# Expert lists of 832 slots, filled by indirect row writes and read transposed, in a chunked-attention and mixture-of-experts kernel

## The chip, the cores and the metric

The kernel runs on one core of one Trainium2 chip. The metric is the time of one execution on the device in microseconds; the kernel before has a median of 394.88 us over three runs (394.33 to 395.27). The core has five engines that run their own instruction streams and wait for each other through semaphores: PE (matrix products into PSUM), DVE and ACT (elementwise work, and the only way out of PSUM), POOL (here mainly the issue of DMAs, among them all indirect ones and all that convert types) and SP (the issue of plain DMAs). All DMAs share 16 DMA engines.

## What is computed

Two stages follow each other. First, attention over chunks of 32 positions with a context of 16 to the left and 8 to the right and 8 memory rows, for 4 batches, 8 heads, 768 positions, 64 channels. Its output, seen as 3072 rows of 512, is the input `x` of a mixture of 8 experts, of which each row uses two.

```
for c in range(nc):                                   # 24 chunks
    k_full = concat([mem_k, k[:, :, l_start:r_end]]); v_full = likewise
    a = softmax(scale * q_c @ k_full^T)
    out[:, :, c_start:c_end] = a @ v_full
...
noisy_logits = x @ w_gate + log1p(exp(x @ w_noise)) * noise
top2 = the two largest of 8; top2_w = softmax over the two
for e in range(E):
    h = relu(x[rows of e] @ w1[e])                    # 512 -> 1024
    out[rows of e] += top2_w * (h @ w2[e])            # 1024 -> 512
```

## The kernel before

The program is written in the order in which each engine executes it (`manual_schedule`); an engine takes its instructions strictly in that order.

**Attention.** It runs over 16 pairs of heads (4 batches of 4 pairs). Loop iteration `i` (L462) works on several pairs at once: transposes of `q` and `k` for pair `i+2` (`qkT_pe`, L206), scores for `i+1`, softmax for `i`, the product with `v` for `i-1` (`PV_pe`, L273), its normalised result written into the row tile `xrow` of the batch (`mult_dve`, L286, L294), transposes of those rows and router logits for `i-2` and `i-3`. The row tile has two buffers, so batch `b` reuses the one of batch `b-2`. The loads of `q`, `k`, `v` (L109, L118) go out on POOL in groups of two pairs, two groups ahead, each into one of three buffers; after the last group POOL issues the first three weight loads (`w1` and `w2` of expert 0, `w1` of expert 1: L439, L444). A weight load reads 2 MB of f32 and writes 1 MB of bf16.

**Routing.** For each batch, `route(b)` (L320) finds the two experts of each row with 8 x 8 comparisons, and counts rows by unordered pair of experts: 28 buckets of up to 128 rows. The rank of a row in its bucket comes from products with a triangular and an all-ones matrix (L368 to L373). One-hot products (L395, L409) turn ranks into a table of row numbers, 128 per bucket. Rows that find no place (rank over 127) go to a spill list of 32, and beyond that to a closing loop (L738) that runs all experts over 128 rows at a time. The rows of each batch, with 8 gate values behind them, are written once to DRAM (`x_rows`, L385, on SP).

**Experts.** A row is gathered once, by bucket (`gather`, L578, an indirect DMA on POOL), transposed on PE (`turn`, L585) and copied into `xTb`, where it stays for both of its experts. Expert `e` uses the seven buckets that contain it: a first product of 32 x (512 + 416) columns (L644), relu shared between ACT and DVE (L630, L632), a second product per bucket of 8 matmuls of 512 columns (L652). The first expert of a bucket stores its scaled result in an SBUF accumulator (L656), the second adds to it on DVE (L659) and writes the 128 rows to `out` by an indirect DMA (L660). The weights of expert `e+2` are issued during expert `e`; `w1` and `w2` have three buffers each. After the last write the closing loop is entered zero times for this input, and the program ends.

## Time and profile before

| What | us |
|---|---|
| median of three runs | 394.88 |
| span of the profiled execution, first to last instruction | 393.1 |
| PE busy | 304.5 (77%) |
| DVE busy | 169.9 (43%) |
| POOL busy | 124.5 (32%) |
| ACT busy | 119.8 (30%) |
| DMA moved | 42.93 MB, 109 GB/s on average |

The profile is one execution on the chip. "Busy" counts the time in which an engine executes, not its waits. A row of the order-of-time view gives start, duration, engine, line, operation and tiles, the number of merged instructions, and in brackets the idle time before it with what ended that. "SPq" and "ACTq" rows are the issue of DMAs. The clock column is the share of PE's full clock that was granted. Times are microseconds from the span's start.

### The profile page before, as it was taken

To read this page: it belongs to the slowest core of one execution; us is meant where nothing else is said; L and a number is where in the kernel's file an instruction comes from. 1 tells how busy PE (TensorE), PEld (TensorE's weight loads), DVE (VectorE), ACT (ScalarE), POOL (GpSimd) and SP (SyncE) were. 2 spreads that over 40 slices of the span, in tenths; PEclk is the share of its full clock that TensorE was granted. 3 is DMA by queue.
4 is the path that set the end of the run, shared out by engine and by line. 5 is a ranking of instruction groups with operands and counts; after the bars stand their busy time and mean duration, and the time that the engine had idled before them with its cause. 6 is when DMAs were issued, how large, how long until landed. Compare 5 with 4: busy or idle time off the path is not lost.

```text
span 393.1 us, 9217 instructions
## 1 busy us (share of the span) xinstructions
PE 304.5 (77%) x4042; PEld 188.6 (48%) x4060; DVE 169.9 (43%) x350; ACT 119.8 (30%) x235; POOL 124.5 (32%) x143
## 2 busy tenths in 40 slices
PE   0448688676846433888998998999998999999990
PEld 0436566454634322654465474454454454544540
DVE  7426345787757761342142242241433242443340
ACT  1436354565532200222333232233221312302200
POOL 7766234265000026352100420520605123032061
PEclk9999555898885655699999999999999999999997
DMA  9999999999970412849700291291492921811021
GB/s 92 100 164 156 158 152 94 167 150 141 211 154 3 143 46 80 151 82 216 141 0 2 45 221 30 64 209 34 97 213 88 191 56 71 132 67 70 3 115 59
DMA packets 83324, 42.93 MB, mean 109 GB/s; under 512 B 57255, under 2 KB 76711, under 8 KB 83280
## 3 DMA queue, kind: packets, MB, share of 16 engines
q0 software_dynamic: 74928, 38.85, 70.6%
q1 hardware_dynamic: 8064, 3.38, 3.4%
q8 instruction: 34, 0.56, 0.6%
q10 hardware_dynamic: 288, 0.07, 0.1%
q14 instruction: 10, 0.08, 0.1%
HBM read 61.32 MB, written 10.65 MB: 183 GB/s over the span
## 4 chain that ended last, share of the span: by engine, by line
PE 60%; DVE 15%; issue 10%; DMA 7%; ACT 3%; POOL 3%; POOLq 0%; DVEq 0%; ACTq 0%
PE ps_h L644 24%; PE ps_y L652 21%; DMA x_rows<-xrow 4%; PE p_t L216 3%; DMA kg<-in_k_dram 2%; PE ps_o L279 2%; PE ps_o L282 2%; DVE xrow L294 2%; PE p_t L589 2%; DVE vg L130 2%; DVE xTb L590 2%; POOL out_dram L660 2%; DVE mx L251 1%; ACT qT L218 1%; PE p_x L303 1%
## 5 line engine op out<-in xcount | busy, mean ns | idle before, releaser
L644 PE MATMUL ps_h<-xTb,w1t 128*128 128x512 bf16 (+3 forms) x608 | 107.8, 328 | 1.1 <-DVE xTb L590 1.0
L652 PE MATMUL ps_y<-w2t,ht 128*128 128x512 bf16 x430 | 98.9, 379 | 1.0 <-issue 0.2
L644 PEld LDWEIGHTS <-w1t 128*128 128x128 bf16 x864 | 64.7, 98 | 45.0 <-issue 1.1
L632 DVE TENSOR_SCALAR ht<-ps_h 128x416 bf16<-128x416 f32 (+2 forms) x68 | 41.7, 613 | 81.0 <-PE ps_h L644 81.0
L660 POOL DMA_INDIRECT out_dram<-acc,sidx x28 | 28.0, 998 | 144.9 <-DVE acc L659 142.4
L652 PEld LDWEIGHTS <-ht 128*128 128x128 bf16 x448 | 42.3, 98 | 48.9
L630 ACT ACTIVATE ht<-ps_h 128x416 bf16<-128x416 f32 (+2 forms) x68 | 36.3, 535 | 87.2 <-PE ps_h L644 83.1
L580 POOL DMA_INDIRECT xl<-x_rows,gidx x28 | 29.1, 1038 | 71.4 <-DVE ov1b L523 48.4
L644 PE MATMUL ps_h<-xTs,w1t 128*128 128x32 bf16 x256 | 45.4, 177 | 0.2 <-DVE xTs L605 0.2
L118 POOL DMA_DIRECT2D vg<-in_v_dram x34 | 32.9, 974 | 35.4 <-PE ps_o L282 29.8
L656 ACT ACTIVATE acc<-ps_y,meta 128x512 f32<-128x512 f32 x28 | 19.2, 687 | 76.5 <-PE ps_y L652 47.7
L659 DVE SCALAR_TENSOR_TENSOR acc<-ps_y,meta,acc 128x512 f32<-128x512 f32 x28 | 21.0, 751 | 38.6 <-PE ps_y L652 38.6
L590 DVE COPY xTb<-p_t 128x512 bf16<-128x512 bf16 x28 | 11.8, 423 | 27.1 <-PE p_t L589 26.9
L218 ACT CAST qT<-p_t 128x384 bf16<-128x384 f32 x32 | 16.9, 586 | 20.2 <-PE p_t L216 20.2
L216 PE MATMUL p_t<-identb,kg 128*64 128x128 bf16 x192 | 14.1, 275 | 10.5 <-ACT qT L218 7.7
L251 DVE TENSOR_REDUCE mx<-ps_s 128x12 f32<-128x768 f32 x16 | 15.2, 950 | 12.1 <-PE ps_s L243 12.1
L305 ACT COPY xt<-p_x 128x768 bf16<-128x768 bf16 x16 | 12.8, 799 | 22.5 <-PE p_x L303 22.5
L216 PE MATMUL p_t<-identb,qg 128*64 128x128 bf16 x192 | 11.5, 265 | 9.5 <-DMA qg<-in_q_dram 5.1
L279 PE MATMUL ps_o<-memv,PT 128*128 128x132 bf16 x96 | 11.2, 273 | 9.4 <-DVE PT L270 9.4
L589 PE MATMUL p_t<-identb,xl 128*128 128x128 bf16 x112 | 11.2, 224 | 8.9 <-DVE xTb L590 8.9
L218 ACT CAST kT<-p_t 128x384 bf16<-128x384 f32 x32 | 17.0, 597 | 2.0 <-PE p_t L216 1.7
L294 DVE TENSOR_TENSOR xrow<-ps_o,rec 128x768 bf16<-128x768 f32 x16 | 15.3, 958 | 5.3 <-DMA x_rows<-xrow 4.8
(128 smaller groups left out, 295.5 us busy)
## 6 DMA issues: line engine op xcount, KB each, us to landing
w1t<-in_moe_w_dram POOLq DMA_DIRECT2D x8, 1024.0 KB
w2t<-in_moe_w_dram POOLq DMA_DIRECT2D x8, 1024.0 KB
vg<-in_v_dram POOLq DMA_DIRECT2D x30, 168.0 KB
x_rows<-xrow SPq DMA_DIRECT2D x3, 792.0 KB, 6.3
qg<-in_q_dram POOLq DMA_DIRECT2D x6, 384.0 KB
kg<-in_k_dram POOLq DMA_DIRECT2D x6, 384.0 KB
qg<-in_q_dram POOLq DMA_DIRECT2D x4, 192.0 KB
kg<-in_k_dram POOLq DMA_DIRECT2D x4, 192.0 KB
```

Of the source, the lines that this page charges most:

```text
L118: nc.gpsimd.dma_start(out=vg[p0 + j:p0 + j + nj, x, c:c + n, hh, :], in_=bass.AP(v.tensor, v.offset + (hd * S + c * chunk + j - left_ctx) ...
L216: nc.tensor.matmul(out=p_t[64 * hh:64 * hh + 64, j, :], lhsT=src[:, 2 * i + hh, (SH * x + j) * D:(SH * x + j + 1) * D], rhs=identb, start= ...
L218: nc.scalar.copy(dst[:, :, SH * x:SH * (x + 1)], p_t.rearrange("d j p -> d p j"))
L294: nc.vector.tensor_tensor(out=xr, in0=po.rearrange("p x (u h) c -> p x u h c", h=2)[:, :, :, :, :D], in1=rec.rearrange("p x (u h o) -> p x ...
L580: nc.gpsimd.indirect_dma_start(out=xl, out_offset=None, in_=xd, in_offset=bass.IndirectOffsetOnAxis(ap=gidx[:, p:p + 1], axis=0), bounds_c ...
L590: nc.vector.tensor_copy(xTv[:, :, p, :], p_t)
L630: nc.scalar.activation(out=dst, in_=src, func=Act.Relu)
L632: nc.vector.tensor_scalar(out=dst, in0=src, scalar1=0.0, scalar2=None, op0=Alu.max)
L644: nc.tensor.matmul(out=ps_h[:, o:o + w], lhsT=w1t[:, kp, f * 128:(f + 1) * 128], rhs=rhs(kp), start=(kp == 0 and i == 0), stop=(kp == KP - ...
L652: nc.tensor.matmul(out=ps_y, lhsT=ht[:, f, j * CAP:(j + 1) * CAP], rhs=w2t[:, f, :], start=(f == 0), stop=(f == FB - 1))
L659: nc.vector.scalar_tensor_tensor(out=a, in0=ps_y, scalar=gate, in1=a, op0=Alu.mult, op1=Alu.add)
L660: nc.gpsimd.indirect_dma_start(out=out_part[p], out_offset=bass.IndirectOffsetOnAxis(ap=sidx[:, p:p + 1], axis=0), in_=a, in_offset=None, ...
```

## The change

The buckets by pair of experts, their tables, the spill list, the gathers of rows and the transposes on PE go. In their place each expert has a list of `CAP` = 832 slots in a DRAM tensor `x_lists`, of rows of 256 + 16 words (the row in bf16, 8 gates, row number, slot number in the second list). Behind the lists lies one slot per row for overflow.

- **Routing** (`s5`): the position of a row in each of its two lists is the count of earlier rows for that expert plus the list's base. The lower position is `offA`, the higher `offB`.
- **Filling** (`s7`): for each tile of 128 rows, two indirect DMAs on POOL write the rows from `xrow` to the lists, 12 for each batch, 48 in all. For batches 0 to 2 they stand in the loop of attention, one iteration after the logits are complete; those of batch 3 stand in the expert stage. At the start, ACT's queue writes zeros over the last 128 slots of each list.
- **Closed slots**: after three batches, the first `SEAL` = 512 slots of lists 0 and 1 are closed; later rows go behind them. They are read right after attention (`load_x`), and the units of expert 0 and 1 that use only them are placed between the routing steps of the last batch (`work`).
- **Reading** (`load_x`): a DMA with transpose on SP reads slots of a list straight into `XT`, 128 channels by 4 by 832; two or three small DMAs read the 16 words behind the rows.
- **Products**: `up` does 2 x 416 columns for each of 32 weight tiles, `down` does six tiles of 128 slots and one of 64 whose two column halves use two column groups of PE.
- **Adding**: every expert writes its rows to `out` by seven indirect DMAs. Before that, rows which another expert has already written are gathered from `out` into the accumulators (`gather`, seven indirect DMAs), which `blank` has set to zero, and `down` adds to them. The gathers for expert `e+1` stand behind the writes of expert `e`; the weight loads for `e+2` behind the gathers for `e`; the second matrix of expert 1 behind the gathers for expert 1.

```diff
-    CAP = 128
-    SPILL = 32
+    CAP = 832
+    SEAL = 512
+    xl_d = nc.dram_tensor("x_lists", [LROWS, ROW], I32, kind="Internal").ap()
+    xl_part = dram_disjoint_views(xl_d, 2 * NP)
+    xp = ctx.enter_context(tc.tile_pool(name="xp", bufs=2))
+    xTp = ctx.enter_context(tc.tile_pool(name="xTp", bufs=3, reuse_waits="tile"))
...
+        zrow = ap_.tile([128, ROW], I32, name="zrow", bufs=1)
+        nc.vector.memset(zrow, 0)
+        for e in range(E):
+            nc.scalar.dma_start(out=xl_d[(e + 1) * CAP - 128:(e + 1) * CAP, :], in_=zrow)
...
+                xrows[b] = xp.tile([128, BT, ROW], I32, name="xrow")
+                nc.gpsimd.memset(xrows[b][:, :, XC + E + 2:], 0)
...
+            def s5():
+                nc.vector.tensor_tensor(out=pos, in0=R["ps_r"][:, :BT, :], in1=bce(base[b]), op=Alu.add)
+                nc.vector.tensor_tensor(out=far, in0=pos, in1=bce(lim), op=Alu.is_ge)
+                nc.vector.scalar_tensor_tensor(out=pos, in0=far, scalar=FAR, in1=pos, op0=Alu.mult, op1=Alu.add)
+                nc.vector.tensor_tensor(out=pos, in0=pos, in1=R["two"], op=Alu.mult)
+                nc.vector.tensor_reduce(out=hi, in_=pos, axis=AX, op=Alu.max)
+                nc.vector.tensor_reduce(out=sm, in_=pos, axis=AX, op=Alu.add)
+                nc.vector.tensor_tensor(out=offA, in0=sm, in1=hi, op=Alu.subtract)
+                nc.vector.tensor_tensor(out=offB, in0=hi, in1=over_at[:, t0:t0 + BT], op=Alu.min)
...
+            def s7(role):
                 for t in range(BT):
+                    sc = nc.gpsimd.indirect_dma_start(
+                        out=xl_part[2 * (t0 + t) + role], out_offset=bass.IndirectOffsetOnAxis(ap=R["off"][role][:, t:t + 1], axis=0),
+                        in_=xrows[b][:, t, :], in_offset=None, bounds_check=LROWS - 1, oob_is_err=False)
...
+        def load_x(e, lo, hi):
+            got = [nc.sync.dma_start(out=XT[e][:, :, lo:hi], in_=xl_x[r0 + lo:r0 + hi, :Dm], transpose=True)]
...
+        def start_route(b):
+            r = route(b)
+            pending.append((r["s1"], r["s2"]))
+            pending.append((r["s3"], r["s4"], r["s5"], r["s6"], lambda: r["s7"](0), lambda: r["s7"](1), r["s8"]))
...
+            if i == NPAIR:
+                load_x(0, 0, SEAL)
+                load_x(1, 0, SEAL)
...
+        def up(e, f, lo, hi):
+            n = 1 if hi - lo <= 512 else 2
+            w = (hi - lo) // n
+            for kp in range(KP):
+                for x in range(n):
+                    nc.tensor.matmul(out=ps[x][:, :w], lhsT=W1[e][:, kp, f * 128:(f + 1) * 128], rhs=XT[e][:, kp, lo + x * w:lo + (x + 1) * w],
+                                     start=(kp == 0), stop=(kp == KP - 1))
+            for x in range(n):
+                relu(HT[e][:, f, lo + x * w:lo + (x + 1) * w], ps[x][:, :w])
...
+        def gather(e, i):
+            nc.gpsimd.indirect_dma_start(
+                out=(a[:, :DH] if last else a).bitcast(I32), out_offset=None, in_=(out_h(out) if last else out).bitcast(I32),
+                in_offset=bass.IndirectOffsetOnAxis(ap=IX[e][1][:, i:i + 1], axis=0),
+                bounds_check=(2 * N if last else N) - 1, oob_is_err=False)
...
+        def down(e, i):
...
+            if e == 0:
+                nc.scalar.activation(out=a[:, :w], in_=ps_y[:, :w], func=Act.Copy, scale=gate)
+            else:
+                nc.vector.scalar_tensor_tensor(out=a[:, :w], in0=ps_y[:, :w], scalar=gate, in1=a[:, :w], op0=Alu.mult, op1=Alu.add)
+            nc.gpsimd.indirect_dma_start(
+                out=out_h(o) if last else o, out_offset=bass.IndirectOffsetOnAxis(ap=IX[e][0][:, i:i + 1], axis=0),
+                in_=a[:, :w], in_offset=None, bounds_check=(2 * N if last else N) - 1, oob_is_err=False)
...
+        r = route(B - 1)
+        r["s1"]()
+        work(2)
+        r["s2"]()
+        work(4)
+        r["s3"]()
+        r["s5"]()
+        r["s4"]()
+        r["s6"]()
+        r["s7"](0)
+        tail_loads.extend(load_x(0, SEAL, CAP))
+        r["s7"](1)
+        load_x(1, SEAL, CAP)
+        load_x(2, 0, CAP)
...
+        work(len(units))
...
+        for f in range(FB):
+            up(0, f, SEAL, CAP)
...
+        for i in range(ST, NT):
+            down(0, i)
+        for i in range(NT):
+            gather(1, i)
+        load_w2(1)
+        load_w1(2)
+        load_w2(2)
...
+        for e in range(1, E):
+            if e + 2 < E:
+                load_x(e + 2, 0, CAP)
+                load_w1(e + 2)
+                load_w2(e + 2)
+            if e > 1:
+                for f in range(FB):
+                    up(e, f, 0, CAP)
...
+            for i in range(NT):
+                down(e, i)
+                if e + 1 < E:
+                    blank(e + 1, i)
+            if e + 1 < E:
+                for i in range(NT):
+                    gather(e + 1, i)
```

The closing loop stays, over the rows whose list was full.

573 lines of the change are left out of this document (231 added, 342 removed).

## The prediction

> **What bounds the kernel now.** I read the page first, then busy time by stage, then POOL and DVE in order of time, then the chain of waits.
>
> ```profile
> span 393.1 us, 9217 instructions
> PE 60%; DVE 15%; issue 10%; DMA 7%; ACT 3%; POOL 3%; POOLq 0%; DVEq 0%; ACTq 0%
> ```
>
> Busy time by stage (length, then each engine's busy time and count, granted clock, DMA share, GB/s moved):
>
> ```profile
> 26.00:133.00 107.00, 74.78 (x2076) 59.95 (x2075) 69.63 (x146) 53.11 (x94) 34.14 (x39) 0.76 1.34 145
> 133.00:157.70 24.70, 7.49 (x172) 5.50 (x171) 12.37 (x59) 1.89 (x6) 9.39 (x10) 0.50 0.21 56
> 157.70:195.50 37.80, 32.56 (x262) 20.36 (x265) 10.73 (x25) 10.37 (x30) 13.76 (x14) 0.93 0.81 149
> 195.50:223.50 28.00, 26.82 (x233) 15.85 (x235) 8.36 (x15) 9.03 (x19) 2.00 (x2) 1.00 0.04 13
> 223.50:357.30 133.80, 130.65 (x983) 68.87 (x993) 45.67 (x74) 34.19 (x66) 36.26 (x37) 1.00 0.55 112
> 357.30:383.10 25.80, 25.69 (x183) 12.76 (x183) 10.83 (x17) 4.46 (x8) 8.00 (x9) 1.00 0.16 62
> 383.10:393.10 10.00, 0.01 (x1) 0.00 (x0) 0.75 (x1) 0.00 (x0) 1.31 (x2) 0.77 0.15 58
> ```
>
> Three stages with three limits. To 133 us attention is a loop of loads, PE and DVE, with the DMA engines busy throughout (145 GB/s). From 133 to 157.7 the last batch is routed and PE is nearly idle. From there PE is full: experts 2 to 6 take 133.8 us, 26.8 each, with PE busy 130.65. The last 10 us are the last write and the end of the program. POOL has 36.26 us of work in those 133.8: it is far from the limit, and the change loads POOL most.
>
> **Prices.** An indirect DMA on POOL, seven in a row, first and last; the first rows landed when ACT could copy them:
>
> ```profile
> 143.89 1.16 POOL L580 DMA_INDIRECT xl<-x_rows,gidx  x1 [48.42 <-DVE ov1b L523]
> ...
> 151.97 1.01 POOL L580 DMA_INDIRECT xl<-x_rows,gidx  x1 [0.30 <-issue]
> 147.04 0.20 ACT L591 COPY meta<-xl 128x8 f32<-128x8 f32 x1 [7.82 <-DMA xl<-x_rows,gidx]
> L660 POOL DMA_INDIRECT out_dram<-acc,sidx x28 | 28.0, 998 | 144.9 <-DVE acc L659 142.4
> ```
>
> Six steps in 8.08 us: 1.31 us of POOL each (1.35 with the first). Writing costs the same 1.0 busy. Landing follows 2.0 us after POOL is done (147.04 less 145.05). A weight load moves 1.05 MB; two of them fill this window at 211 GB/s, so 5.0 us each:
>
> ```profile
> 256.00:266.00 10.00, 9.95 (x83) 5.72 (x83) 3.75 (x6) 3.26 (x6) 1.85 (x2) 1.00 1.13 211
> 130.00:132.00 2.00, 1.05 (x34) 0.71 (x32) 0.55 (x2) 0.80 (x1) 0.00 (x0) 1.00 1.02 340
> ```
>
> The second row is a row write alone, at 340 GB/s. POOL may also hold back an issue:
>
> ```profile
> 15.20 0.78 POOL L109 DMA_DIRECT2D qg<-in_q_dram  x1
> 15.98 0.78 POOL L109 DMA_DIRECT2D kg<-in_k_dram  x1
> 16.73 3.95 POOL L118 DMA_DIRECT2D vg<-in_v_dram  x4
> 20.64 0.82 POOL L109 DMA_DIRECT2D qg<-in_q_dram  x1
> 21.42 0.82 POOL L109 DMA_DIRECT2D kg<-in_k_dram  x1
> 23.37 1.02 POOL L118 DMA_DIRECT2D vg<-in_v_dram  x1 [1.14 <-DMA qg<-in_q_dram]
> ```
>
> The load at 23.37 waits for a q load that it shares no data with: the one issued eight places before. So I take it that POOL keeps eight transfers open.
>
> **Start.** Eight zero-row writes go on ACT's queue ahead of the `mem_k` loads.
>
> ```profile
> 0.84 1.65 ACTq L151 DMA_DIRECT2D mk_nat<-in_mem_k_dram  x4
> 12.27 0.63 PE L199 MATMUL p_m<-ident,mk_nat 32*128 32x32 f32 x4 [12.27 <-DVE ident L178]
> 22.74 0.85 PE L216 MATMUL p_t<-identb,qg 128*64 128x128 bf16 x12 [5.06 <-DMA qg<-in_q_dram]
> x_rows<-xrow SPq DMA_DIRECT2D x3, 792.0 KB, 6.3
> ```
>
> They wait for DVE's memsets (about 11 us), issue in 8 x 0.41, and move 1.1 MB beside the first loads (by 792 KB in 6.3: 9 us). `mem_k` then lands near 20 instead of under 12. PE has 5 us of idle time at 22.74 that absorb most. I take +3; bounds 0 (all hidden) and +9 (none).
>
> **Attention.** Twelve writes per batch at 1.31 are 15.7 us on POOL, in the middle of its loads, and the row buffer is free only when all twelve land.
>
> ```profile
> 67.85 0.78 POOL L109 DMA_DIRECT2D qg<-in_q_dram  x1
> 93.03 0.80 POOL L439 DMA_DIRECT2D w1t<-in_moe_w_dram  x1
> 73.73 0.96 DVE L294 TENSOR_TENSOR xrow<-ps_o,rec 128x768 bf16<-128x768 f32 x1
> 85.26 0.96 DVE L294 TENSOR_TENSOR xrow<-ps_o,rec 128x768 bf16<-128x768 f32 x1
> 90.45 0.96 DVE L294 TENSOR_TENSOR xrow<-ps_o,rec 128x768 bf16<-128x768 f32 x1
> 115.03 0.96 DVE L294 TENSOR_TENSOR xrow<-ps_o,rec 128x768 bf16<-128x768 f32 x1 [4.02 <-DMA x_rows<-xrow]
> 127.27 0.96 DVE L294 TENSOR_TENSOR xrow<-ps_o,rec 128x768 bf16<-128x768 f32 x1
> ```
>
> Batch 0's rows and slots are ready after pair 6 (73.73 + 0.96 + 3 for the start + about 15 small DVE operations of 0.2): 80.8. The writes end at 96.5 and land at 98.5, and pair 8, which reuses the buffer, runs then, not at 85.26: **+13**. The q and k of pair 12, issued at 67.85 now, go out behind the writes at 96.5 and land near 102.5; PE stops for them, and pair 9 comes at 106.5: +16. The last two groups' loads (2.9 MB at 145 GB/s, 20 us) run to 118, and three weight loads, issued at 109 instead of 93, to 133. Batch 1's writes start at 119.5, but the eighth is eight places behind the third weight load: it starts at 133, the twelfth ends at 139.5 and lands at 141.5. Pair 12 runs then instead of at 115.03: +26.5. Pair 14 follows 12.2 later as now, 153.7; batch 2's slots are ready at 158, its writes end at 173.5 and land at 175.5.
>
> **First experts.** Now the transposed read of 512 rows, 0.52 MB. No row shows one. Near rows: 576 KB written plainly, 3.3 us; 792 KB beside weight loads, 14.1.
>
> ```profile
> 100.86 14.07 DMA x_rows<-xrow
> 128.25 3.34 DMA x_rows<-xrow
> ```
>
> I take 5, near the plain one, as little else moves then; bounds 3 and 14. The Trainium skill ("Advanced Engine Details and Errata", X-Bar Transpose) calls transposing DMAs as fast as plain ones; by that alone the sum would fall by 2 us, and no run here shows it yet. The first expert matmul is then at 180.5, against 157.7 (**+23**): the gap of 24.7 us that routing leaves today is not closed but moved, and table building, 112 transposes and their copies are what goes.
>
> ```profile
> 157.69 6.32 PE L644 MATMUL ps_h<-xTb,w1t 128*128 128x256 bf16 x32 [0.52 <-DVE xTb L590]
> 165.76 3.67 PE L644 MATMUL ps_h<-xTb,w1t 128*128 128x256 bf16 x32 [0.52 <-DVE xTb L590]
> 344.96 3.18 PE L652 MATMUL ps_y<-w2t,ht 128*128 128x512 bf16 x14
> ```
>
> PE starts cold (the same 32 matmuls 6.32 against 3.67; a full one is 0.215). Six units of four full matmuls stand before the last batch's ranking on PE: 5.1 + 2.9 cold, to 188.5. Ranking and slots 3.8, writes of the first expert's rows 7.9, landing 2, the 320 remaining rows 4 by the same pace: 206. Work in between lasts to 200.5 and is hidden. Remaining rows up and down with a cold start, 10.6, then a write and its landing: 220.5, when the gathers for expert 1 may start. They take 9.2, and the second matrix of expert 1 is issued **behind** them, at 230; it lands at 236.5, while PE is ready at 224 (216.5 and 7.7 for the rest of expert 1's first product). Its second product takes 11.2 and 2.5 cold: expert 1 ends at 250, where today it ends at 223.5.
>
> **Later experts.** PE's work falls: 64 matmuls of 416 columns (0.175 each), 48 full and 16 half ones in two column groups: 11.2 + 10.3 + 0.9 = 22.4 us, against 26.8. But POOL must do 14 indirect DMAs and two weight loads, 14 x 1.31 + 1.8 = 20.1, and a gather for the next expert waits until all seven writes of this one landed. In order: gathers 9.2, weight loads issued, first bytes 1 later, 10 to move, then the writes that queue behind them (1.7 MB at 340 GB/s, 5), landing 2: **27.2 us** a period. Bounds 22.4 (PE alone) and 32 (transposed reads add 5). Expert 1's writes stand behind five weight loads (25 us from 231), so the gathers for expert 2 start at 263. Four periods to expert 6: 372. No weights then: 22.4, 394.5. First rows 3.3, the last products 8.5: 406. With the 10 us of today's end, span 416 against 393.1. The median lies 1.8 above the span (394.88): **418 us**.
>
> **Rivals.**
> *The queue does not hold writes behind weights.* Then batch 1's writes land 4 us sooner, and experts 2 to 7 run at PE's 22.4 (133.8 against 159.6). 246 + 133.8 + 10 + 1.8 = 391, faster by 1%. It decides once the period is below 26.6 less the front's loss spread over six, 22.9. For it: the DMA share is 0.55 in today's expert stage. Against: POOL's eight open transfers put the next expert's first gather eight places behind the second weight load. The Trainium skill ("DMA: Bandwidth & Descriptors", Queues, rings and completion order) says that an engine takes one ring's descriptors in order and alternates only between rings; by it the writes do wait and 418 stands; no row of before shows it, since nothing there waits for a small transfer behind a weight load.
> *Transposed reads are slow*, 14 us for 512 rows as the contended write: +9 and +7 before the first gathers, +2 in each period: 418 + 16 + 8 = 442. For it: they compete with weights in every period.
> *Attention does not pay*: only the start and the tail of the writes show, first expert matmul near 161: 398. Against: POOL works in order, and 24 of the 36 writes stand ahead of loads or weights.
> *The lists overflow* and the closing loop runs a pass over all experts: the reference's own routing of this draw gives 715 to 808 tokens an expert, below 832; 2 in 100.
>
> **How the numbers follow.** Forecast 0.50, slow transposes 0.20, free queue 0.18, free attention 0.10, overflow 0.02. The forecast's own range, from start 0 to +9, period 25 to 30: 403 to 434. To leave out no more than 2 in 10 the range takes in the free queue and slow transposes: 389 to 444. Faster 0.19 (free queue and a little), same 0.03, slower 0.78; 0.2% is about what a measurement of this kernel can tell from no change.
>
> **What would show it.** Pair 8's product near 98 and pair 12's near 141, both waiting for list writes; the first expert matmul near 180 after the transposed read; a PE gap before expert 1's second product, waiting for its weights; PE idle some 5 us per later expert, waiting through DVE for a gather. PE without gaps from 250 on, or a first expert matmul before 170, would prove me wrong.

## The result and the profile after

The changed kernel takes 448.76 us (median of four, 444.53 to 453.05); the kernel before, run beside it, 395.07. The ratio is 1.132, with a 95% interval of 1.126 to 1.138. The forecast was 418 with a range up to 444: the direction was right, the size was not, by 30 us of span (446.4 against 416).

The first fence is the page of the kernel after: span, busy time of each engine, and two of the costliest groups (busy time and mean of one, then the idle time before them with what ended it).

```profile
span 446.4 us, 7962 instructions
PE 288.7 (65%) x3247; PEld 168.7 (38%) x3257; DVE 175.6 (39%) x403; ACT 108.0 (24%) x202; POOL 219.9 (49%) x245
...
L604 PE MATMUL ps_y<-w2t,ht 128*128 128x512 bf16 x375 | 92.5, 403 | 31.5 <-DMA w2t<-in_moe_w_dram 17.8
L590 POOL DMA_INDIRECT acc<-out_dram,gi x49 | 49.9, 1018 | 64.1 <-issue 60.2
```

PE has less to do than before (288.7 against 304.5 us) and POOL much more (219.9 against 124.5). Yet POOL is busy for only half of the span: no engine is full. The time lies in waits in line, which the stages show (length, busy time of the engines with counts, granted clock, DMA share, GB/s):

```profile
26.00:160.00 134.00, 84.47 (x2107) 66.34 (x2106) 67.23 (x142) 55.72 (x100) 59.01 (x67) 0.69 1.17 120
160.00:187.00 27.00, 7.13 (x62) 3.96 (x64) 5.51 (x24) 2.73 (x6) 12.12 (x12) 0.50 0.40 103
187.00:230.00 43.00, 34.45 (x172) 16.59 (x173) 11.02 (x47) 15.31 (x28) 18.66 (x19) 0.90 0.54 135
230.00:275.75 45.75, 27.67 (x151) 14.28 (x152) 14.15 (x34) 6.71 (x14) 18.48 (x20) 0.81 0.93 177
275.75:305.80 30.05, 23.31 (x137) 11.47 (x136) 11.50 (x26) 3.40 (x7) 15.94 (x16) 0.89 0.80 170
420.00:446.40 26.40, 10.31 (x60) 4.81 (x57) 4.99 (x7) 0.00 (x0) 10.97 (x11) 0.77 0.33 110
```

Attention ended at 133 before and the first expert matmul came at 157.7; now pair 15 is done at 166 and that matmul comes at 183. The row 275.75 to 305.80 is one later expert: 30 us with PE busy for 23.3, where the kernel before needed 26.8 with PE full. The last row is the end, just behind the start of the last gathers (416.15): PE is busy for 10.3 of its 26.4 us.

POOL in order of time, in the same kernel:

```profile
136.72 0.98 POOL L420 DMA_INDIRECT x_lists<-xrow,offB  x1 [3.83 <-DMA w1t<-in_moe_w_dram]
230.15 1.07 POOL L590 DMA_INDIRECT acc<-out_dram,gi  x1 [3.24 <-DVE ht L545]
239.12 0.99 POOL L444 DMA_DIRECT2D w2t<-in_moe_w_dram  x1
266.04 0.98 POOL L612 DMA_INDIRECT out_dram<-acc,wi  x1 [1.71 <-DMA w1t<-in_moe_w_dram]
275.75 1.05 POOL L590 DMA_INDIRECT acc<-out_dram,gi  x1 [8.72 <-issue]
285.51 0.99 POOL L444 DMA_DIRECT2D w2t<-in_moe_w_dram  x1
286.96 1.08 POOL L612 DMA_INDIRECT out_dram<-acc,wi  x1 [0.46 <-DVE acc L610]
294.83 0.98 POOL L612 DMA_INDIRECT out_dram<-acc,wi  x1 [0.31 <-issue]
305.81 1.05 POOL L590 DMA_INDIRECT acc<-out_dram,gi  x1 [9.99 <-issue]
427.78 1.03 POOL L612 DMA_INDIRECT out_dram<-acc,wi  x1 [2.68 <-DVE acc L610]
435.57 0.98 POOL L612 DMA_INDIRECT out_dram<-acc,wi  x1 [0.30 <-issue]
```

The rows of L590 are the first of seven gathers for experts 1, 2 and 3 (called G1, G2, G3 from here on; the rest follow at 336.3, 365.4, 394.0 and 416.2). Before G2 and G3 POOL stands still for 8.72 and 9.99 us after its last write: the writes are issued (between 286.96 and 295.81 before G3), but have not landed. "issue" means that the view names no releaser. The DMA packets of the same trace, which it holds with their times and sizes, tell more: a load of `w1` is 512 packets of 2048 bytes, one of `w2` 1024 of 1024 bytes, and written rows go mostly in packets of 4096.

| Period from | gathers end | packets of the two loads | written rows' last packet | next first gather |
|---|---|---|---|---|
| G2 | 284.70 | 286.26 to 298.83 | 304.03 | 305.81 |
| G3 | 314.76 | 316.31 to 329.15 | 334.44 | 336.29 |
| G4 | 345.24 | 346.89 to 359.13 | 363.28 | 365.44 |
| G5 | 374.39 | 375.95 to 388.78 | 392.36 | 393.96 |

The first packet of the written rows follows at 298.05, 327.78, 358.50 and 387.48, as the loads end: the weight loads lie ahead of the writes in the queue. In the last expert no weights are loaded, yet seven writes come after seven gathers on POOL: the last is issued at 435.57.

PE, DVE and ACT in order of time, same kernel:

```profile
104.61 0.96 DVE L320 TENSOR_TENSOR xrow<-ps_o,rec 128x768 bf16<-128x768 f32 x1 [0.23 <-DVE rec L319]
144.68 0.96 DVE L320 TENSOR_TENSOR xrow<-ps_o,rec 128x768 bf16<-128x768 f32 x1 [0.38 <-POOL xrow L315]
183.31 0.58 PE L555 MATMUL ps_h<-xT,w1t 128*128 128x512 bf16 x1 [13.22 <-DMA xT<-x_lists]
209.96 0.16 DVE L576 TENSOR_TENSOR tk<-mt,times 128x3 f32<-128x3 int32 x1 [10.83 <-DMA mt<-x_lists]
217.02 0.44 ACT L543 ACTIVATE ht<-ps_h 128x320 bf16<-128x320 f32 x1 [6.36 <-remote]
250.35 0.59 PE L604 MATMUL ps_y<-w2t,ht 128*128 128x512 bf16 x1 [17.81 <-DMA w2t<-in_moe_w_dram]
```

These are the product of pair 8, that of pair 12, the first expert matmul, the row numbers of the last tiles of expert 0, a relu for the same tiles, which ACT starts after 6.36 us of standing still ("remote": a releaser that the profile does not hold), and the second product of expert 1, which waits 17.8 us for its weights.

### The profile page after: what moved, and what is told of

Read it like the earlier page. It is cut to its first block, busy times and chain, and to the rows that moved or that the text cites. A ratio compares the mean times of both kernels' runs of the same rounds, so it can differ in the third digit from the quotient of the medians.

```text
span 446.4 us, 7962 instructions
## 1 busy us (share of the span) xinstructions
PE 288.7 (65%) x3247; PEld 168.7 (38%) x3257; DVE 175.6 (39%) x403; ACT 108.0 (24%) x202; POOL 219.9 (49%) x245
## 5 line engine op out<-in xcount | busy, mean ns | idle before, releaser
L604 PE MATMUL ps_y<-w2t,ht 128*128 128x512 bf16 x375 | 92.5, 403 | 31.5 <-DMA w2t<-in_moe_w_dram 17.8
L590 POOL DMA_INDIRECT acc<-out_dram,gi x49 | 49.9, 1018 | 64.1 <-issue 60.2
L612 POOL DMA_INDIRECT out_dram<-acc,wi x56 | 55.9, 998 | 44.7 <-DVE acc L610 20.7
L555 PE MATMUL ps_g<-xT,w1t 128*128 128x416 bf16 (+2 forms) x280 | 64.6, 346 | 13.2 <-issue 6.4
L555 PE MATMUL ps_h<-xT,w1t 128*128 128x416 bf16 (+2 forms) x231 | 58.6, 359 | 16.7 <-DMA xT<-x_lists 13.2
L610 DVE SCALAR_TENSOR_TENSOR acc<-ps_y,mt,acc 128x512 f32<-128x512 f32 (+1 forms) x49 | 34.0, 695 | 63.4 <-PE ps_y L604 37.9
L420 POOL DMA_INDIRECT x_lists<-xrow,offA x24 | 23.9, 996 | 60.7 <-issue 25.4
L543 ACT ACTIVATE ht<-ps_g 128x416 bf16<-128x416 f32 (+2 forms) x44 | 21.9, 511 | 115.8 <-PE ps_g L555 69.4
L121 POOL DMA_DIRECT2D vg<-in_v_dram x34 | 33.0, 976 | 27.9 <-PE ps_o L307 20.9
L545 DVE TENSOR_SCALAR ht<-ps_g 128x416 bf16<-128x416 f32 (+2 forms) x26 | 15.0, 579 | 38.9 <-PE ps_g L555 27.1
L420 POOL DMA_INDIRECT x_lists<-xrow,offB x24 | 23.9, 996 | 10.8 <-issue 5.5
L265 PE MATMUL ps_s<-kT,qT 64*32 64x56 bf16 (+2 forms) x768 | 14.8, 213 | 21.5 <-issue 20.9
L331 ACT COPY xt<-p_x 128x768 bf16<-128x768 bf16 x16 | 12.8, 799 | 54.8 <-PE p_x L329 53.9
L563 DVE MEMSET acc<- 128x512 f32 x49 | 23.8, 485 | 2.9 <-issue 0.3
L265 PEld LDWEIGHTS <-qT 64*32 64x32 bf16 x768 | 10.3, 99 | 24.5 <-issue 24.2
```

The source lines that it names most:

```text
L121: nc.gpsimd.dma_start(out=vg[p0 + j:p0 + j + nj, x, c:c + n, hh, :], in_=bass.AP(v.tensor, v.offset + (hd * S + c * chunk + j - left_ctx) ...
L265: nc.tensor.matmul(out=o[:, lo:hi], lhsT=qT[hs, chunk * c:chunk * (c + 1)], rhs=kT[hs, k0 + lo:k0 + hi], start=True, stop=True)
L420: sc = nc.gpsimd.indirect_dma_start(out=xl_part[2 * (t0 + t) + role], out_offset=bass.IndirectOffsetOnAxis(ap=R["off"][role][:, t:t + 1], ...
L543: nc.scalar.activation(out=dst, in_=src, func=Act.Relu)
L555: nc.tensor.matmul(out=ps[x][:, :w], lhsT=W1[e][:, kp, f * 128:(f + 1) * 128], rhs=XT[e][:, kp, lo + x * w:lo + (x + 1) * w], start=(kp == ...
L563: nc.vector.memset(a, 0.0)
```

## The experiments

Each run was made beside the kernel before, which took 386.8 to 394.6 us on the chips used, so ratios to it are compared, and points in time. The times of best_b and spread are medians of four runs, that of reads of ten, the others single runs. The ratio of a single run is good to about 1%: the changed kernel itself gave 1.132 and, once more (`after_b`), 1.140.

| Run | us | ratio | what it is |
|---|---|---|---|
| no_wait | 404.11 | 1.041 | gathers free of the writes |
| no_weights | 412.32 | 1.062 | five experts without weight loads |
| no_x | 438.95 | 1.131 | five experts without transposed reads |
| order | 434.69 | 1.120 | weight loads behind the writes |
| split | 436.59 | 1.106 | one load ahead of them, one behind |
| w2early | 437.70 | 1.132 | expert 1's second matrix earlier |
| zlate | 439.87 | 1.137 | zero rows later |
| bufs4 | 437.86 | 1.132 | four row tiles |
| defer | 437.06 | 1.130 | and list writes behind the loads |
| pad | 441.83 | 1.120 | and zeroing on DVE |
| after_b | 442.19 | 1.140 | the changed kernel again |
| calm | 415.07 | 1.071 | pad, list writes last in program order |
| best, best_b | 414.29, 398.19 | 1.050, 1.026 (1.020 to 1.032) | all parts |
| spread | 399.82 | 1.031 | all parts, writes in threes |
| reads | 390.13 | 1.003 (0.999 to 1.008) | all parts, reads early |

### What fills the period of an expert

**no_wait.** Experts 0 to 6 write their rows to tensors of their own and the gathers read `q` instead, so that no gather waits for a write; the sum of a row's two experts is left out. All transfers stay.

```diff
-    out_part = dram_disjoint_views(out, E * NT)
+    out_part = []
+    for e in range(E):
+        dst = out if e == E - 1 else nc.dram_tensor(f"y_rows{e}", [N, Dm], F32, kind="Internal").ap()
+        out_part += list(dram_disjoint_views(dst, NT))
```

> Part left out: the sum of a row's two experts. Experts 0 to 6 write to tensors of their own, only expert 7 to the output, and the gathers read the same number of rows from q, so no gather waits for the writes of the expert before; every transfer, its size and its place in the queue stay. Theory 'chain' (a period of 29.6 us is gathers 9.2, weight loads 12, the seven writes behind them 5, landing 3, one after the other, because the next gather waits for the landing): without the wait, POOL (20.1 us a period) and PE (22.4) set the pace, periods near 23, total 448 - 4 x 6.6 = about 420. Rival 'traffic' (63 MB instead of 43 MB saturate the DMA engines whatever the order): periods stay at 28 to 30, total 440 to 448.

Measured: POOL in order of time, the first gathers for three experts in a row, the `w2` load ahead of the second, and the last gather and first write of expert 6, behind which no load stands.

```profile
257.83 1.05 POOL L594 DMA_INDIRECT acc<-in_q_dram,gi  x1 [4.44 <-DMA w2t<-in_moe_w_dram]
267.57 0.98 POOL L448 DMA_DIRECT2D w2t<-in_moe_w_dram  x1
281.77 1.05 POOL L594 DMA_INDIRECT acc<-in_q_dram,gi  x1 [4.07 <-DMA w2t<-in_moe_w_dram]
305.56 1.05 POOL L594 DMA_INDIRECT acc<-in_q_dram,gi  x1 [3.91 <-DMA w2t<-in_moe_w_dram]
...
362.21 1.01 POOL L594 DMA_INDIRECT acc<-in_q_dram,gi  x1 [0.30 <-DVE acc L614]
363.52 1.02 POOL L616 DMA_INDIRECT y_rows<-acc,wi  x1 [0.30 <-issue]
```

The period falls from 29.6 to 24.1 us (mean of four) with every byte still moved, and the ratio to 1.041, where the expected 420 us would be about 1.06. So the bytes are not the limit; that the gathers wait for the writes of the expert ahead is. What is left is above PE's 22.4 us: each first gather stands eight places behind a `w2` load on POOL and waits for it to land, 14.2 us after its issue (267.57 to 281.77). The last two rows show one more wait by its absence: the first write follows the last gather at once (0.30 us). In the changed kernel no load stands between the two for experts 6 and 7 either, and yet the write comes 2.4 and 2.7 us after: there it goes to the tensor that the gathers read, and waits until they have landed.

**no_weights** and **no_x** take one thing out of the later experts each: experts 3 to 7 compute with the weights that lie in the buffers already, or with the rows that lie there. So ten weight loads are left out in the one and five transposed reads in the other.

```diff
-                load_w1(e + 2)
-                load_w2(e + 2)
+                W1[e + 2], W2[e + 2] = W1[e - 1], W2[e - 1]
```

```diff
+                XT[e] = xTp.tile([128, KP, CAP], BF16, name="xT") if e < 3 else XT[e - 3]
...
+            got = [nc.sync.dma_start(out=XT[e][:, :, lo:hi], in_=xl_x[r0 + lo:r0 + hi, :Dm], transpose=True)] if e < 3 else []
```

> Part left out: experts 3 to 7 use the weights of the expert three before; ten weight loads fall away, everything else stays. Theory 'chain': gathers 9.2, writes 9.2, landing 2 to 3 make 21 us, so PE's 22.4 sets the period, as between experts 6 and 7 where no loads stand (22.2 measured); the gathers for expert 2 start some 5 us sooner; total 448 - 4 x 7 - 5 = about 415. If the period stayed over 26, the weight loads are not what the writes wait behind.

> Part left out: experts 3 to 7 use the transposed rows of the expert three before; the small reads behind the rows stay. Theory 'chain': the transposed reads run on another queue and cost the period only what they take from weight loads beside them: 28 to 29.6 us a period, total 442 to 448. Rival 'traffic': 0.85 of some 6.4 MB a period less, 29.6 x 0.87 = 25.7, total about 432.

Measured: without weights the periods are 25.6, 24.4, 26.0, 22.6 and 22.6 us (22.4 was expected), without the reads still 28.9 on average. The first three of no_weights each hold the transposed read of a later expert, and POOL stands still for 4.2 to 6.1 us between their last gather and first write, in the two others 2.1. A period of no_weights, POOL in order of time, from the last gather to the next first one:

```profile
347.59 1.00 POOL L590 DMA_INDIRECT acc<-out_dram,gi  x1 [0.30 <-issue]
350.73 1.02 POOL L612 DMA_INDIRECT out_dram<-acc,wi  x1 [2.14 <-DVE acc L563]
...
358.51 0.98 POOL L612 DMA_INDIRECT out_dram<-acc,wi  x1 [0.30 <-DVE ht L545]
362.25 1.06 POOL L590 DMA_INDIRECT acc<-out_dram,gi  x1 [2.76 <-issue]
```

This is the chain bare: gathers 9 us, 2.1 until they have landed (the first rows were added at 345.95, and the writes still waited), writes 8.8, 2.8 to land. It is 22.6 us long without any weights. With both loads ahead of the writes the last wait is 8.4 to 10.0 us instead of 2.8. The Trainium skill ("DMA: Bandwidth & Descriptors", Queues, rings and completion order) says of the queues of SP and ACT that a DMA engine consumes their descriptors in ring order. The trace agrees, for POOL's queue (loads to 298.83, rows from 298.05 on, and a wait of 9.99 against 2.76 us).

**order** puts both loads behind the writes, **split** one ahead (`w1`) and one behind (`w2`; its edit is shown). Both compute the whole result.

```diff
             if e + 2 < E:
                 load_x(e + 2, 0, CAP)
                 load_w1(e + 2)
-                load_w2(e + 2)
...
             if e + 1 < E:
+                if e + 2 < E:
+                    load_w2(e + 2)
                 for i in range(NT):
                     gather(e + 1, i)
```

> The result is complete. The two weight loads of expert e+2 stand behind the seven writes of expert e instead of ahead of them, still ahead of the gathers for e+1. Theory 'chain': the writes land 3 us after their issue, but the gathers' data now come behind 12 us of weights; writes 11 after the first rows, weights 12, rows 1.5: periods of about 25.5, total 448 - 4 x 4 + 4 = about 436. Rival 'traffic': the same bytes, 29.6 a period, total 448.

> The loads of expert e+2 are parted: w1 stays ahead of the writes of expert e, w2 goes behind them. Chain theory (what stands on POOL's queue ahead of the writes is paid in full, a load takes 5 to 6 us): without any weights a period was 22.5 to 26 us, with both loads behind the writes 28.1, with both ahead 29.6. One load of 5.5 us lies beside the gathers' data and the adds, the other beside the writes' landing, so about half of both is hidden: periods 24 to 26 us, sum of four 18 us less than in the changed kernel, total ratio about 1.08. Rival (the 2.1 MB of an expert take their time wherever they stand, because the queue's transfers follow one another): periods stay at 28 to 29.6 and the ratio at 1.12 to 1.13.

Measured: order has 29.4, 26.7, 29.0 and 27.4 us a period. The writes land at once, but the gathers' rows now lie behind two loads, and POOL stands still for 6.8 to 7.9 us between the last gather and the first write. The expected 25.5 was missed; and from G6 to G7, where the changed kernel needs 22.2 us, order needs 27.5, since the loads for expert 7 now stand there. Split has 25.2, 32.5, 25.8 and 23.9: three of four as the theory says, one not. So the place of a load in the line decides what it costs, and with one on either side about half of the 4.9 us that both cost (29.6 against 24.6 without) is hidden. What made one period long (a transposed read takes 11 us on SP's queue in it) was left for the last run.

**w2early** issues `w2` of expert 1 right after the list writes of the last batch.

```diff
         r["s7"](1)
+        load_w2(1)
         load_x(1, SEAL, CAP)
...
-        load_w2(1)
```

> The result is complete. The second matrix of expert 1 is loaded behind the last batch's list writes, ahead of the gathers for expert 1. PE's wait of 17.8 us for it goes. Theory 'chain': the writes of expert 1 still queue behind four weight loads, so the gathers for expert 2 start only about 5 us sooner (275.75 to near 270), and the total falls by 5. Rival: PE's wait is on the path in full, the total falls by 15 or more.

Measured: PE's wait of 17.8 us is gone, G2 begins 40.4 us after G1 (45.6 in the changed kernel), and the ratio is the same within the scatter. Of the wait of 17.8 us that the page puts first, 5 lay on the path, as the theory had it. POOL at G2:

```profile
267.89 1.05 POOL L590 DMA_INDIRECT acc<-out_dram,gi  x1 [10.06 <-issue]
```

The last write of expert 1 was issued at 256.85, 9 us sooner than in the changed kernel, and then waited behind four loads to land.

### What holds the attention up

**zlate** issues the eight zero-row writes behind the `mem_k` loads on ACT's queue.

```diff
-        for e in range(E):
-            nc.scalar.dma_start(out=xl_d[(e + 1) * CAP - 128:(e + 1) * CAP, :], in_=zrow)
...
             nc.scalar.dma_start(out=mk_nat[b * n_mem:(b + 1) * n_mem], in_=mem_k[b].rearrange("h m d -> m h d"))
+        for e in range(E):
+            nc.scalar.dma_start(out=xl_d[(e + 1) * CAP - 128:(e + 1) * CAP, :], in_=zrow)
```

> The result is complete. The eight zero-row writes on ACT's queue stand behind the loads of mem_k instead of ahead of them. Theory: the first pair's product comes 4 us sooner (36.7 to near 33) and everything behind it too, first expert matmul near 180, total 3 to 4 us less. Rival: the 1.1 MB beside the first loads cost the time, in whatever order: no change.

Measured: pair 0's product at 33.80, against 36.70 in the changed kernel and 35.83 to 36.96 in the three runs on the same chip; the total within the scatter of one run. Against the kernel before (32.34) the start costs 4.4 us, where the forecast had 3, and this order takes back 2 to 3 of them.

**bufs4** gives each batch a row tile of its own; **defer** does that too and moves the list writes of batches 0 and 1 behind the last `q`, `k`, `v` loads and `w1` of expert 0, and the next two weight loads behind batch 2's writes.

```diff
-    xp = ctx.enter_context(tc.tile_pool(name="xp", bufs=2))
+    xp = ctx.enter_context(tc.tile_pool(name="xp", bufs=4))
```

```diff
-            pending.append((r["s3"], r["s4"], r["s5"], r["s6"], lambda: r["s7"](0), lambda: r["s7"](1), r["s8"]))
+            fills.append(r)
+            pending.append((r["s3"], r["s4"], r["s5"], r["s6"], r["s8"]))
...
+            if i >= GP * (NG - 3) + 1 and i % HP == HP - 1:
+                while fills and not pending:
+                    r = fills.pop(0)
+                    r["s7"](0)
+                    r["s7"](1)
+                if i == NPAIR - 1:
+                    load_w2(0)
+                    load_w1(1)
```

> The result is complete. Four row tiles instead of two, so no pair waits until the list writes of an earlier batch have landed; POOL's order is as it was. Theory 'order': most of the loss in attention is that the loads of q and k for pair 12 stand behind the twelve writes of batch 0; pair 8's product comes near 92 us (104.6 with two tiles), but pair 9 still waits for those loads (near 107), and only the second wait, of pair 12 for batch 1's landing, goes: first expert matmul near 175 instead of 183.3. Rival 'buffer': the reuse of the row tile is the whole loss; first expert matmul near 163.

> The result is complete. Four row tiles, and the writes of batches 0 and 1 stand on POOL behind the last loads of q, k, v and the first weight load; the other two early weight loads stand behind the writes of batch 2. Theory 'order': attention then keeps the pace of the kernel before, plus 4 us of the start; batch 2's slots are ready near 133, its writes end near 150, first expert matmul near 157 to 160 instead of 183.3, and the total falls by as much, 23 to 26 us. If the first expert matmul stayed over 170, something else than POOL's order slows attention.

Measured, bufs4: pair 8 comes at 90.38 without waiting, and pair 9 at 107.69 as before, because `q` of pair 12 is late. PE in order of time:

```profile
103.01 0.85 PE L241 MATMUL p_t<-identb,qg 128*64 128x128 bf16 x12 [10.34 <-DMA qg<-in_q_dram]
```

Measured, defer: no pair waits up to pair 13 (122.39), then pair 14 comes only at 140.57; and the lists, complete at 161, are read late. PE and SP in order of time:

```profile
132.80 0.71 PE L329 MATMUL p_x<-identb,xrow 128*128 128x128 bf16 x5 [9.65 <-POOL xrow L315]
162.35 11.80 SPq L454 DMA_TRANSPOSE xT<-x_lists  x1
178.88 0.59 PE L564 MATMUL ps_h<-xT,w1t 128*128 128x512 bf16 x1 [27.80 <-DMA xT<-x_lists]
```

L315 zeroes the last words of a row tile on POOL, an instruction of 0.15 us. It stands behind 24 writes, and a pair needs it. And the transposed read of 512 rows, 4.4 us from issue to use in the changed kernel (178.93 to 183.31), takes 16.5 with two weight loads beside it.

**pad** is defer with that zeroing on DVE and the two loads ahead of batch 2's writes. **best** is pad with zlate, split, and `w2` of expert 1, `w1` and `w2` of expert 2 issued when the first expert's rows have landed.

```diff
-                nc.gpsimd.memset(xrows[b][:, :, XC + E + 2:], 0)
+                nc.vector.memset(xrows[b][:, :, XC + E + 2:], 0)
...
+        nc.gpsimd.tensor_copy(landed, XT[0][:, 0, :1])
+        load_w2(1)
+        load_w1(2)
+        load_w2(2)
```

> The writes of batches 0 and 1 stand behind the last q, k, v loads and w1(0), as in the run before; new are the zeroing of a row's last words on VectorE instead of POOL, and w2(0), w1(1) ahead of batch 2's writes instead of behind them. Theory (in that run pair 14 waited because POOL zeroes the last words of batch 3's rows, and this instruction stood behind 24 writes): pair 14's product comes 4 to 8 us after pair 13's, at 127 to 131, pair 15's at 134 to 138, batch 2's writes start at 133 to 138 instead of 145. Theory of the transposed read (16 us because two weight loads ran beside it): the first expert matmul comes 5 to 7 us after the last write of batch 2 is issued, at about 155 to 162; the total 12 to 20 us less, ratio 1.08 to 1.10. Rivals: the stall of pair 14 is one of SCALAR's queue and stays (pair 14 at 140); the read waits for the writes' landing and not for the loads (18 us after the writes, first matmul past 168).

> All parts together: rows in four tiles, zeroing on VectorE, writes of batches 0 and 1 behind the last q, k, v loads, w2(0) and w1(1) ahead of batch 2's writes, the zero rows behind the loads of the memory keys, w2(1), w1(2), w2(2) right after the first expert's rows landed, and of each later expert w1 ahead of the writes and w2 behind them. Chain theory: first expert matmul at 152 to 160; G1 at 197 to 207; G1 to G2 27 to 33 us, since only one load (w1 of expert 3) stands ahead of the writes, where five did (45.6 us); five periods of 24 to 25; G7 at 345 to 362; 30 us to the end: 376 to 392, ratio 0.975 to 1.015. Rival (the parts hide one another, as each of them alone left the total where it was): 405 to 425.

Measured: both missed what was expected, pad at 1.120 and best in the range of its rival. In the expert stage the parts did their work: G1 to G2 takes 23.5 us instead of 45.6 in best, as one load stands ahead of the writes instead of five, though three of its periods stay at 27.1 to 30.5; and the read after the writes of batch 2 takes 4.5 us again in pad. In the attention they did not: pair 15 at 163.5 and 162.4. In both, PE's scores trickled while the lists were written. The waits of PE in best from 95 to 165 us, and PE in order of time:

```profile
PE ps_s L265 <- issue: 19.9, 24, 1.9
```

```profile
125.86 0.25 PE L265 MATMUL ps_s<-kT,qT 64*32 64x56 bf16 x4 [1.19 <-issue]
127.26 0.26 PE L265 MATMUL ps_s<-kT,qT 64*32 64x56 bf16 x4 [1.15 <-issue]
```

Four matmuls, then a pause for which the view names no releaser: 24 of them, 0.8 us on average. The first profile of the changed kernel has the same (20.9 us in 23 pauses), and so have split and pad; the eight others so far have under 1.5 us of it. The next four runs, on one chip, ask whether this is the loss.

**after_b** is the changed kernel unedited. **calm** is pad with all 36 list writes of batches 0 to 2 behind the last pair in program order (and three routing tiles).

```diff
+            if i == NPAIR:
+                for r in fills:
+                    r["s7"](0)
+                    r["s7"](1)
```

> The changed kernel once more, for a profile beside the next three on one chip. In its first profile TensorE's scores (ps_s) sat idle 20.9 us in 23 pauses for nothing that the profile shows, all while writes of the lists ran; the same stretch of the runs with before near 387 us shows under 1.5 us of it, and waits for the buffers of the rows (12 to 16 us, twice) in its place. Theory (two covers for one loss: the writes hold the pairs 8 and 12 up by some 15 us each, by the buffer where the scores do not pause): the products of pairs 8 and 12 come at 95 to 106 and 140 to 146 again, whichever of the two shows; ratio 1.12 to 1.14. Rival (the pauses are a loss of their own): without the pauses pair 15 comes 10 us or more ahead of 165.

> All 36 writes of batches 0 to 2 stand behind the attention (rows in four tiles, routing tiles in three, zeroing on VectorE), w2(0) and w1(1) ahead of them. It measures what the writes cost the attention. Theory (the writes beside it cost it 25 to 30 us): pair 15's product at 132 to 142 (131.7 before the change, 165.4 with it), the idle time of ps_s for nothing shown under 3 us; the writes then take 46 us in one piece, from about 143 to 190, first expert matmul at 194 to 200, ratio 1.14 to 1.18. Rival (the attention is slower for another reason: the zero rows, the longer route): pair 15 past 150.

Measured, after_b: no pauses (0.8 us), and the attention is no faster; the waits that the forecast named stand in their place. DVE in order of time:

```profile
98.86 0.96 DVE L320 TENSOR_TENSOR xrow<-ps_o,rec 128x768 bf16<-128x768 f32 x1 [8.54 <-DMA x_lists<-xrow,offB]
144.19 0.96 DVE L320 TENSOR_TENSOR xrow<-ps_o,rec 128x768 bf16<-128x768 f32 x1 [16.68 <-POOL xrow L315]
```

Pair 8 waits for the list writes to land (98.86), pair 12 for the zeroing behind them. Pair 15 is at 165.4 with the pauses and at 163.5 without: in the changed kernel the one loss covers the other.

Measured, calm: a miss that taught most. POOL does not wait for the place in the program: its writes, last in order, had their data, and ran from 96.8 to 152.3, beside the attention. POOL and PE in order of time:

```profile
105.40 0.98 POOL L420 DMA_INDIRECT x_lists<-xrow,offA  x1 [2.29 <-DMA w1t<-in_moe_w_dram]
110.27 0.98 POOL L420 DMA_INDIRECT x_lists<-xrow,offB  x1 [3.89 <-DMA w2t<-in_moe_w_dram]
158.46 0.59 PE L564 MATMUL ps_h<-xT,w1t 128*128 128x512 bf16 x1 [22.81 <-DMA xT<-x_lists]
```

Pair 15 is at 132.11, where it was before the change (131.69), with some 20 of the 36 writes issued beside it. So on this chip the writes as such cost the attention nothing; what cost it 31 us (163.5 to 132.1) was what stood behind them on POOL: the loads of `q`, `k`, `v`, the zeroing, and the row tile. The total falls by 27 us against after_b.

**best_b** is best again, and timed; **spread** issues the list writes three at a time after each pair from pair 7 on.

```diff
+            for _ in range(min(len(fills), 3 if i < NPAIR - 1 else 36)):
+                fills.pop(0)()
+            if i == NPAIR - 2:
+                load_w2(0)
+                load_w1(1)
```

> The kernel with all parts together, once more and timed. Theory (the pauses of the scores during the writes come with the chip and take what the parts gain in the attention): where the scores pause, pair 15's product at 160 to 165 and the ratio at 1.04 to 1.06 as in the first run; where they do not, pair 15 at 138 to 146, first expert matmul at 158 to 166, G1 15 us earlier, ratio 0.99 to 1.02. Rival (the attention is held for another reason): pair 15 past 155 without pauses.

> As the one above, but the writes of batches 0 to 2 are issued three at a time after each pair from pair 7 on, instead of twelve to 24 in one piece. Theory (the scores pause while a row of writes is in flight, about 1.2 us for each few matmuls, and recover in between): 3.9 us of writes in each 6 to 7 us, pauses of 1 to 2 us a pair, pair 15 at 140 to 152, and the total 5 to 15 us under the one above where the scores pause. Rival (a pause for each write, however they are placed; or the q, k, v loads, now behind three writes each, come late): pair 15 at 158 or later, the total the same or more.

Measured: best_b without pauses has pair 15 at 133.8, the first expert matmul at 157.9, G1 at 206.3, and 398.19 us, where 0.99 to 1.02 was expected; spread has 137.4, 156.0, 206.0 and, over four executions, 394.8 to 411.3. Parting the writes gains nothing that shows on this chip, which has no pauses; whether it does where there are some was not tried.

**reads** gives the rows of experts 3 to 7 five tiles of their own and issues their transposed reads right behind that of expert 2.

```diff
-        load_x(2, 0, CAP)
+        for e in range(2, E):
+            load_x(e, 0, CAP)
...
-                load_x(e + 2, 0, CAP)
```

> All parts together, and the transposed reads of experts 3 to 7 go into five tiles of their own and are issued right behind those of expert 2, in the stretch before the first gathers, instead of one at the start of each later expert. In the run before, three periods took 29.7, 30.2 and 32.4 us, each with one of these reads beside the gathers (7.4, 6.1 and 6.6 us on SyncE's queue) and 9 to 11 us from the last gather to the first write; the two periods without a read took 24.2 and 23.2. Theory (the reads beside the gathers hold their data up): all periods 23 to 26 us, 15 us less from G2 to G5, the reads' 25 us in the stretch from 190 to 215 costing 0 to 8 us before G1; 380 to 392, ratio 0.98 to 1.01 where the parts together stood at 1.026. Rival (it is the loads of w2 behind the writes that hold the gathers up): periods 2 to 4 stay at 29 to 32, and the total is the same or more.

Measured: busy time from one first gather to the next, G1 to G5 (columns as above), and the last two reads on SP:

```profile
203.80:236.80 33.00, 27.01 (x148) 13.46 (x147) 12.84 (x32) 5.83 (x12) 15.80 (x16) 0.97 1.16 181
236.80:266.10 29.30, 15.16 (x95) 7.25 (x95) 10.13 (x23) 1.03 (x2) 15.85 (x17) 0.69 1.07 161
266.10:289.50 23.40, 23.40 (x134) 12.06 (x133) 12.55 (x27) 5.19 (x11) 15.82 (x17) 1.00 0.84 185
289.50:312.50 23.00, 23.00 (x132) 11.79 (x131) 12.79 (x27) 5.24 (x11) 15.76 (x16) 1.00 0.90 192
```

```profile
212.57 11.68 SPq L455 DMA_TRANSPOSE xT<-x_lists  x1
228.93 17.54 SPq L455 DMA_TRANSPOSE xT<-x_lists  x1
```

The long periods moved with the reads: the two that now hold the last reads (212 to 246) take 33 and 29 us, and the next three 23, with PE full and a `w2` load behind the writes as before. So transposed reads beside gathers cost a period 6 us and more; the rival (the `w2` loads) falls. It fits that no_weights has its long periods where a read stands, and that no_x gained only 0.6 us a period: there the writes waited behind two loads anyway. In split the other periods hold a read too and are short, so a read does not always cost that much. The total, 390.13, is level with the kernel before (388.1).

## Why the prediction was wrong

Up to the last expert, the chain that the prediction drew is the one that ran; one term of it, the price of a weight load, was too small, and the end lacked a step. Forecast points against those of the profile after:

| Point | forecast | measured |
|---|---|---|
| pair 8, pair 9 | 98.5, 106.5 | 104.6, 109.1 |
| pair 12, pair 14 | 141.5, 153.7 | 144.7, 157.2 |
| first expert matmul | 180.5 | 183.3 |
| G1 | 220.5 | 230.2 |
| G2 | 263 | 275.8 |
| G6, after four periods | 372 | 394.0 |
| G7 | 394.5 | 416.2 |
| end of the span | 416 | 446.4 |

- **Start and attention: right** (2.8 us of the miss). The wait of pair 8 for the list writes, the late `q` of pair 12, the write held eight places behind a weight load (136.72), and the tail after batch 2 came where they were put. In the first profile PE's pauses stand in front of pair 8's wait; after_b shows the wait itself, at 98.86 (98.5 in the forecast). One step was missing: the zeroing at L315 on POOL, which the text never named; pad and calm show that it had to go too. It came at the same time as the row tile's release, so the sum did not feel it.
- **The transposed read: right** where it counted, 4.4 us against 5 taken. The Trainium skill ("Advanced Engine Details and Errata", X-Bar Transpose) calls such reads as fast as plain ones. With little beside it this one nearly was (512 KB in 4.4 us, a plain write of 576 KB in 3.3); beside two weight loads it took 16.5 (defer).
- **First experts, G1: 6.8 us too short** (46.8 against 40). The last rows of expert 0 came in time: their first product starts 25.6 us after the first expert matmul, 25.5 in the forecast. Behind that ACT stands still for the 6.36 us shown above. In after_b, the same kernel, it does not, and the step takes 42.1 us, although DVE waits 10.83 us for the small reads behind the rows in both. So some 4.7 us belong to the one execution, for a reason that stays open, and 2.1 to the sum, mostly for landing (3.2 and 3.7 us instead of 2).
- **G1 to G2: 3.1 us too short** (45.6 against 42.5), **and the period: 29.6 against 27.2, 9.2 us in four.** Behind both is the step that failed most, the price of a weight load. The packets give each term of the period, as means of four:

| Term | forecast | measured |
|---|---|---|
| seven gathers | 9.2 | 9.0 |
| to the first packet of the loads | 1 | 1.6 |
| two weight loads | 10 | 12.6 |
| the written rows behind them | 5 | 4.6 |
| landing, up to the next gather | 2 | 1.8 |

The order of the terms was right, and so was every term but the loads. Their 5.0 us each came from the window 256 to 266 before the change. It does not hold two loads alone: 0.41 of its 2.11 MB are gathered rows (96 packets of 4224 bytes), and the two loads in question, issued at 251.99 and 257.02, moved from 253.7 to 268.0, 14.3 us; the next two such pairs took 13.6 and 12.8. Five loads ahead of expert 1's writes took 29.4 us (240.80 to 270.19) instead of 25. That POOL must issue seven writes, 8.8 us, is indeed covered by the loads: the last was issued 2.6 to 3.2 us before they ended. The upper bound of 32 held, but for another reason than its own: the transposed reads add 0.6 (no_x), not 5.

- **The end: 8.5 us too short** (30.3 from G7 against 21.8), a step left out. The sum had the first rows 3.3 and the last products 8.5 after G7, and then today's 10 us. But the last expert's writes wait on POOL until its seven gathers have landed: they end at 425.1, and the writes go from 427.78 to 436.55, though the first rows were added at 421.5. So the last write ends 6.2 us after the last product (430.3), where it was 2.1 before. Of the rest, 2.4 us are products that came later than forecast, and 1.9 lie between the last write and the end (9.9 us against 8.0 before), which no run explains.

The rivals. *Free queue* (391) fell: the written rows move only as the loads end, and with the loads moved or taken out the periods fall by 1.4 (order) to 4.9 us (no_weights). *Slow transposed reads* (442) came near the time for a wrong reason: leaving them out of the later experts gains 0.6 us each. Only when the loads are out of the way does the read show (no_weights, reads). *Attention free* (398) was wrong for this order, and right as a possibility: calm has it, with the same writes. *Overflow* did not happen: behind the last write, at 435.57, the trace holds no instruction of the closing loop's body.

## What to carry to other kernels

An engine that issues transfers is a line, and its share of busy time says nothing about what a place in that line costs: list what stands behind each long series of indirect transfers, down to a memset of 0.15 us, and what their landing waits behind. In a chain of read, add, write from one step to the next, count for every transfer its issue, its place in the queue and its landing, and put bulk loads where neither side of the chain follows them. Price a load by the time from its first to its last packet, not by the rate of a window that other transfers share: here that was 6.3 us instead of 5.0, and it repeats in every step. Mend such waits together: each of four repairs alone left the ratio at 1.13, because the next wait in line took over, and together they took the kernel back to level with the one before.

## What was not expected of the hardware

- In all four profiles of list-writing kernels from the chips on which the kernel before took 394.6 to 395.1 us, PE's small score matmuls (64 x 32 weights, 56 columns) paused after every three to five, 23 or 24 times, for 17.6 to 20.9 us in all, while list writes were in flight; in the thirteen profiles from chips where it took 386.8 to 388.2 there were at most 1.4 us of it. The same four show 28 to 41 us of waits of DVE and ACT that end with a "remote" releaser, the thirteen none. The profile of the kernel before, from a chip of the first kind, has no such pause and 1.0 us of such waits. Best took 414.29 us on the one kind and 398.19 on the other. What the engines wait for, the trace does not show; it stays open.
- A transposed read of 512 rows took 4.4 us with little beside it and 16.5 beside two weight loads; on SP's own queue the issue of one of 832 rows grew from 3.1 to 17.5 us beside gathers and loads.
- POOL's hold on an issue until the transfer eight places ahead has landed shows again: in calm three writes wait 2.29, 3.89 and 4.04 us for three weight loads that they share no data with, and in no_wait it sets the period.
